# An attention and mixture-of-experts kernel on one core: memory of the last values apart, and the head of the first list gathered from a view without the last two chunks

## The chip, the cores and the metric

The kernel runs on one core of one Trainium2 chip. The metric is the device time of one execution in microseconds (us), as the median of several runs. Of the kernel before three runs are shown, and one more execution was recorded by the hardware profiler; all times of single instructions come from that one.

## The reference

```python
def _attn_ref(q, k, v, tau):                       # q, k, v: 4 x 5056 x 256
    qn = q / (np.linalg.norm(q, axis=1, keepdims=True) + 1e-06)
    kn = k / (np.linalg.norm(k, axis=1, keepdims=True) + 1e-06)
    s = kn.transpose(0, 2, 1) @ qn / tau           # 256 x 256 for each batch
    s = s - s.max(-1, keepdims=True)
    a = np.exp(s)
    a /= a.sum(-1, keepdims=True) + 1e-09
    return v @ a

def _moe_ref(x, w_gate, w1, w2):                   # x: the 20224 rows of the attention's output
    ...
    order = np.argsort(-flat)                      # flat: logits x @ w_gate, 20224 x 8
    assigned = -np.ones(N, dtype=np.int64)
    counts = np.zeros(E, dtype=np.int64)
    for idx in order:                              # each expert takes at most cap = 2528 tokens
        tok, e = (int(idx) // E, int(idx) % E)
        if assigned[tok] >= 0 or counts[e] >= cap:
            continue
        assigned[tok] = e
        counts[e] += 1
    ...
    for e in range(E):
        mask = assigned == e
        h = np.maximum(x[mask] @ w1[e], 0.0)       # 256 -> 1024
        out[mask] = h @ w2[e]                      # 1024 -> 256
```

## The kernel before

**Attention.** The tokens of a batch lie in five chunks of 1024 rows. The function `scores` multiplies keys and queries, `softmax` makes the 256 x 256 matrix a, and the value matmuls (`x_tiles`, L226, tile `px`) make the rows x = v a. One call of `x_tiles` makes a pair of 128-row tiles: matmuls into one PSUM tile `px` (pool `ps_x`, four buffers) and an eviction on ScalarE (L230). Every second pair, `store_x` (L236) stores 512 KB of rows to the DRAM tile `x_d` on ScalarE's queue. The values lie in SBUF tiles `vr` (pool `vp`, nine buffers) or in `ua` and `ub`, which later hold the experts' weights (`HOMES`).

**Routing.** The choice of tokens doesn't read `x_d`: the logits are made from values and gates on the chip and stand in L. For each expert p, `route(p)` finds the tokens: a search over the sixteen high bits of the keys and one over the low bits, four rounds each. A round is a comparison on VectorE (L635, two halves), matmuls that count (L600, L613) and some small steps on VectorE. It ends in a 0/1 mask over 128 x 160 positions, its running sum (`prefix`, L515) and the expert's number `ei`, which starts the load of the expert's weights. `compact(p)` turns the mask into a list of 20 columns of 128 token numbers: per column one matmul (L815, tile `pi`), and one test on ScalarE (L833) or VectorE (L849), for expert 0 in the ratio 11 to 9 (`NACT`); then a dozen very small steps on VectorE make `src` (the rows in `x_d`, last write L917) and `idx` (the rows of the output, L930). A column of the list is gathered by one indirect DMA of GpSimd (`fetch` in `load_x`, L1118, tile `xg`), 128 rows at a time.

**Experts.** Expert by expert, `layer1` (L1316, tile `ph`) and `layer2` (L1350, tile `py`) run over chunks of up to four columns; expert 0 has chunks of 2, 4, 4, 4, 4 and 2 columns (`FIRST_CUT`). Every number is split into a high and a low part, so that three matmuls stand for one: ScalarE writes the high part (L1319), VectorE the low part (L1324). The gathered rows are turned by `turn` (transposes L1273, one PSUM tile `pt`; high part L1275, low part L1278). Most chunks behind the third are turned through DRAM instead (`stage`, L1182 and L1184). A column's result goes from `y` to the output by an indirect DMA (L1359).

**Order.** From the value matmuls of the table `TODO` on the order on all engines is fixed by hand. An object `o` keeps a planned time of TensorE and VectorE; each matmul adds to it (`tick`), and at each tick streams of routing work put their next instruction into the queues when it is due. `o.until(key)` lets that planned time run on, without matmuls, until a stream has reached a point.

**The seam.** `TODO` names 13 chunks of four pairs, 52 pairs in all; the routing of expert 0 and the beginning of that of expert 1 run beside them. Behind them the value pools are closed and the pool `ffx` takes their place. Then the first six columns are gathered: the DRAM tile `x_d` is their source, so each gather waits for all stores. A row of 24 matmuls (L1411, `START_TICKS`) whose results nobody reads is put in TensorE's queue, then `turn(0, 0, 0)` and `turn(0, 0, 1)`, then `layer1` of the first chunk, the two turns of the second chunk, and `layer2` of the first chunk.

## Time and profile before

| what | us |
| --- | --- |
| median of three runs | 1281.18 (1277.91 to 1281.96) |
| the profiled execution, whole | 1281.94 |
| its span, first to last instruction | 1279.2 |
| TensorE busy within the span | 1253.7 |
| VectorE, ScalarE, GpSimd busy | 842.8, 551.0, 395.1 |

A busy time is the sum of the intervals in which an engine had an instruction under way. The span is made of stages with different limits, so the shares of the whole page are averages; the rows below are from the stage around the change, where the value matmuls end and the experts begin. A row of a timeline gives start, length, engine, line, operation, what is written from what, the form, and in brackets how long the engine stood idle before and what ended that. The start of a DMA row is that of the instruction that issues it. The granted clock of TensorE is 1.00 at 2.4 GHz and 0.50 at 1.2 GHz.

### The profile page before, as it was taken

The numbers are of one execution on the slowest core, as the hardware profiler recorded it, in microseconds if no ns is written. First come the engines' busy times: TensorE is split into PE (matmuls) and PEld (weight loads), VectorE is DVE, ScalarE is ACT, GpSimd is POOL, SyncE is SP. The second block draws the span as 40 slices with busy tenths as digits, with TensorE's granted clock in tenths as the row PEclk, the third lists the DMA queues.
The fourth block names the chain that finished last, engine by engine and source line by source line (L and its number), as shares of the span: only waits on it lengthen the run. The fifth ranks groups of instructions, "written<-read, shape, count | busy, mean of one in ns | idle before, by whom it ended". The sixth has DMA issues, their size and how long they took to land.

```text
span 1279.2 us, 23255 instructions
## 1 busy us (share of the span) xinstructions
PE 1253.7 (98%) x8827; PEld 1117.8 (87%) x8827; DVE 842.8 (66%) x2153; ACT 551.0 (43%) x1273; POOL 395.1 (31%) x662
## 2 busy tenths in 40 slices
PE   7999999999899999999999999999999999999998
PEld 6889877888788888998999898988988998898998
DVE  6788595889479678878866877877744334434421
ACT  5567642335234443524443553453455334334331
POOL 1000000000243363244424533453344344335322
PEclk9999999999899999999999999999999999999999
DMA  8998983344224124222422431433143235323310
GB/s 290 364 391 318 394 305 127 132 155 179 67 84 151 38 67 139 84 92 65 157 67 87 148 107 36 147 122 97 64 155 120 78 104 163 106 66 103 111 62 33
DMA packets 67119, 178.29 MB, mean 139 GB/s; under 512 B 10944, under 2 KB 33344, under 8 KB 62400
## 3 DMA queue, kind: packets, MB, share of 16 engines
q1 hardware_dynamic: 39808, 97.54, 21.5%
q0 software_dynamic: 17664, 58.22, 14.1%
q10 hardware_dynamic: 9536, 21.06, 4.2%
q8 instruction: 69, 1.13, 0.4%
q14 instruction: 42, 0.34, 0.1%
HBM read 117.53 MB, written 59.24 MB: 138 GB/s over the span
## 4 chain that ended last, share of the span: by engine, by line
PE 85%; issue 5%; DVE 5%; POOL 2%; DMA 2%; ACT 1%; POOLq 0%; SPq 0%; DVEq 0%; ACTq 0%
PE py L1350 31%; PE ph L1316 30%; PE s L305 8%; PE px L226 8%; PE pc L600 2%; PE px L269 2%; PE px L417 1%; POOL out_dram L1359 1%; DMA xg<-x_d,src 1%; DVE acc_q L315 1%; DVE acc_k L315 1%; DVE hL L1324 1%; PE pi L815 1%; DMA ua<-in_q_dram 1%; ACT hH L1319 0%
## 5 line engine op out<-in xcount | busy, mean ns | idle before, releaser
L1350 PE MATMUL py<-ua,hH 128*128 128x256 f32 (+1 forms) x2560 | 449.9, 279 | 0.0
L1316 PE MATMUL ph<-xH,ua 128*128 128x512 f32 (+3 forms) x1312 | 410.9, 388 | 3.9 <-DVE hL L1324 2.1
L1350 PEld LDWEIGHTS py<-ua,hH 128*128 128x128 f32 (+1 forms) x2560 | 388.5, 187 | 2.3
L1350 PE MATMUL py<-ua,hL 128*128 128x256 f32 (+1 forms) x1280 | 356.6, 279 | 0.0
L1324 DVE SCALAR_TENSOR_TENSOR hL<-ph,hH 128x512 fp32r<-128x512 f32 (+3 forms) x328 | 218.8, 668 | 160.1 <-ACT hH L1319 150.8
L1316 PEld LDWEIGHTS ph<-xH,ua 128*128 128x128 f32 x1312 | 244.6, 189 | 51.3 <-DVE hL L1324 4.4
L1319 ACT ACTIVATE hH<-ph 128x512 fp32r<-128x512 f32 (+3 forms) x328 | 190.8, 582 | 220.2 <-PE ph L1316 210.8
L1359 POOL DMA_INDIRECT out_dram<-y,idx x160 | 158.8, 993 | 319.9 <-ACT y L1357 281.0
L1316 PE MATMUL ph<-xL,ua 128*128 128x512 f32 (+3 forms) x656 | 254.6, 388 | 1.0 <-DVE xL L1278 0.6
L1350 PEld LDWEIGHTS py<-ua,hL 128*128 128x128 f32 (+1 forms) x1280 | 239.2, 187 | 0.0
L1118 POOL DMA_INDIRECT xg<-x_d,src x160 | 163.3, 1021 | 98.1 <-issue 45.6
L1357 ACT ACTIVATE y<-py 128x256 f32<-128x256 f32 (+1 forms) x160 | 61.4, 384 | 287.6 <-PE py L1350 247.6
L305 PE MATMUL s<-ua 128*128 128x256 f32 (+1 forms) x640 | 145.9, 387 | 6.9 <-DMA ua<-in_q_dram 6.9
L305 PEld LDWEIGHTS s<-ua 128*128 128x128 f32 (+1 forms) x640 | 122.4, 194 | 27.0 <-issue 6.4
L1316 PEld LDWEIGHTS ph<-xL,ua 128*128 128x128 f32 x656 | 124.1, 189 | 24.7 <-DVE xL L1278 2.0
L314 ACT ACTIVATE sq<-ua 128x1024 f32<-128x1024 f32 (+1 forms) x80 | 76.3, 970 | 50.4 <-DMA ua<-in_k_dram 19.3
L1204 DVE TENSOR_TENSOR xL<-xT,xH 128x512 fp32r<-128x512 f32 (+1 forms) x68 | 44.9, 678 | 64.4 <-ACT xH L1201 55.8
L1129 POOL COPY spacer<-hH 1x1 f32<-1x1 f32 x128 | 26.8, 209 | 160.8 <-ACT hH L1319 155.1
L230 ACT ACTIVATE xs<-px 128x512 f32<-128x512 f32 x60 | 35.8, 597 | 62.9 <-PE px L226 62.8
L226 PE MATMUL px<-a,vr 128*128 128x256 f32 x256 | 59.0, 384 | 0.0
L335 POOL TENSOR_SCALAR ny<-ny 128x4 f32<-128x4 f32 x4 | 2.0, 506 | 183.5 <-ACT ny L334 183.5
L226 PEld LDWEIGHTS px<-a,vr 128*128 128x128 f32 x256 | 47.1, 190 | 5.8
(298 smaller groups left out, 1358.1 us busy)
## 6 DMA issues: line engine op xcount, KB each, us to landing
x_d<-xs ACTq DMA_DIRECT2D x39, 512.0 KB
ua<-in_k_dram SPq DMA_DIRECT2D x35, 512.0 KB
ua<-in_q_dram SPq DMA_DIRECT2D x35, 512.0 KB
via<-xs SPq DMA_DIRECT2D x33, 512.0 KB
xT<-via SPq DMA_DIRECT2D x132, 128.0 KB
vr<-in_vt_dram SPq DMA_DIRECT2D x14, 1024.0 KB
ua<-in_vt_dram SPq DMA_DIRECT2D x4, 1024.0 KB
xg<-x_d,src POOLq DMA_INDIRECT x160
```

The source lines that it names most:

```text
L226: mm = PE.matmul(px[:, i * C:i * C + width], lhsT=vs[b, c][:, kb, t + i, :], rhs=a_f[b][:, kb, 0:width], start=(kb == 0), stop=(kb == 1))
L230: S.activation(xs[:, t % TH:t % TH + n, 0:width], px[:, 0:n * width].rearrange("p (t c) -> p t c", t=n), AF.Copy)
L305: newest[0] = PE.matmul(sb[:, ib * C:(ib + 1) * C], lhsT=kt[:np_, t, ib * 128:(ib + 1) * 128], rhs=qt[:np_, t, :], start=(first and t == 0 ...
L314: S.activation(sq[:n, t0:t1], t_[:n, t0:t1], AF.Square)
L1118: P.indirect_dma_start(out=xg[:n, i, :], out_offset=None, in_=x_d, in_offset=bass.IndirectOffsetOnAxis(ap=idx[:n, col:col + 1], axis=0))
L1204: V.tensor_tensor(xL[:, kb, 0:k * 128].rearrange("p (i t e) -> p i t e", i=k, t=4), rows, xH[:, kb, 0:k * 128].rearrange("p (i t e) -> p i ...
L1316: PE.matmul(ph[:, 0:nt], lhsT=l[:, w], rhs=x_[:, kb, 0:nt], start=(i == 0), stop=(i == 5))
L1319: S.activation(hH[:, fb, 0:nt], ph[:, 0:nt], AF.Relu)
L1324: V.scalar_tensor_tensor(hL[:, fb, 0:nt], ph[:, 0:nt], 0.0, hH[:, fb, 0:nt].bitcast(F32), op0=OP.max, op1=OP.subtract)
L1350: PE.matmul(py[:n, 0:C], lhsT=l[:, fb, tk], rhs=w[:, d], start=(j == 0), stop=(j == 23))
L1357: S.activation(y[:n], py[:n, 0:C], AF.Copy)
L1359: sd = P.indirect_dma_start(out=out, out_offset=bass.IndirectOffsetOnAxis(ap=idx[:n, col:col + 1], axis=0), in_=y[:n], in_offset=None)
```

## The change

Of the 52 pairs the last six (`LATE`) are put behind the end of the list of expert 0 in TensorE's queue. They belong to the chunks (3, 3) and (3, 4), which now come last in `TODO`; `ua` holds (2, 4) to (3, 2) in their place. These two chunks have value tiles of their own in a pool `vp_l`, and with them the row buffers `xs`, the matrices of the last two batches and two of the four `px` buffers are in pools that stay open (`apool_l`, `vp_l`, `ps_xl`). The other value pools are closed ahead of the last six pairs, `vp` has seven buffers and not nine, and `ffx` is opened in their place.

The list of expert 0 is made in two halves. For the first, `compact` copies the mask, clears its last 16 positions (those of the two late chunks), and makes four columns (`HEAD`) from it, with two tests on ScalarE and two on VectorE. Then it takes the 512 tokens that were listed out of the mask, and makes the other 16 columns (nine tests on ScalarE, seven on VectorE). The four columns of the head are gathered from `x_d[0:LATE_ROW]`, a view that ends ahead of the two late chunks. In TensorE's queue the order is now: five late pairs, the transposes of the first chunk in one PSUM tile (`turn_both`), the sixth pair, `layer1` of the first chunk, `layer2` of its first column, and the two turns of the second chunk within the second column. The 24 matmuls without a reader are gone. The fifth and sixth column are gathered behind the last pair from the whole of `x_d`. The tiles `hH` and `hL` of every second chunk, and the tiles of `stage`, move to a pool `ffx2` in the memory of the late values. For all experts the running sum of the mask moves from `route` to the head of `compact`, behind `ei`.

```diff
...
+LATE = 6
+LATE_ROW = (B * NCH - 2) * CH
...
+HEAD = 4
+NACT = {HEAD: 2, NCOL - HEAD: 9}
...
-BUFS_V = 9
+BUFS_V = 7
...
-         (3, 0): [(2, 2)], (3, 1): [(2, 3)], (3, 4): [(2, 4), (3, 0), (3, 1), (3, 2), (3, 3), (3, 4)]}
+         (3, 0): [(2, 2)], (3, 1): [(2, 3)], (3, 4): [(3, 3), (3, 4), (2, 4), (3, 0), (3, 1), (3, 2)]}
...
+    apool_l = lctx.enter_context(tc.tile_pool(name="apool_l", bufs=1, side="right"))
+    vp_l = lctx.enter_context(tc.tile_pool(name="vp_l", bufs=2, side="right"))
+    ps_xl = lctx.enter_context(tc.tile_pool(name="ps_xl", bufs=2, space=PSUM, side="right"))
...
-    ps_x = actx.enter_context(tc.tile_pool(name="ps_x", bufs=4, space=PSUM, side="right"))
+    ps_x = actx.enter_context(tc.tile_pool(name="ps_x", bufs=2, space=PSUM, side="right"))
...
+    def next_px():
+        px_at[0] += 1
+        return (ps_x if px_at[0] % 2 and px_at[1] else ps_xl).tile([128, 512], F32, name="px")
...
-        yield ve(COLS, 0.5)
-        r["sc"] = prefix(r["mask"], "a")
...
     def compact(p):
+        mask = routed[p]["mask"]
+        if p > 0:
+            yield ve(COLS, 0.5)
+            sc = prefix(mask, "a")
+            yield from listed(p, sc, 0, NCOL)
+            return
+        head = rtile("mem")
+        yield ve(COLS)
+        V.tensor_copy(head, mask)
+        yield ve(16)
+        V.memset(head[:, COLS - 16:COLS], 0.0)
+        yield ve(COLS, 0.5)
+        sc = prefix(head, "a")
+        yield from listed(p, sc, 0, HEAD)
+        yield ve(COLS, 2, ptr=1)
+        V.tensor_scalar(sc, sc, routed[p]["first"], None, op0=OP.add)
+        yield ve(COLS)
+        V.scalar_tensor_tensor(head, sc, HEAD * 128.0, head, op0=OP.is_le, op1=OP.mult)
+        yield ve(COLS)
+        V.tensor_tensor(head, mask, head, op=OP.subtract)
+        yield ve(COLS, 0.5)
+        sc = prefix(head, "a")
+        yield from listed(p, sc, HEAD, NCOL)
+
+    def listed(p, sc, c0, c1):
...
-            P.indirect_dma_start(out=xg[:n, i, :], out_offset=None, in_=x_d,
-                                 in_offset=bass.IndirectOffsetOnAxis(ap=idx[:n, col:col + 1], axis=0))
+            rows = x_d[0:LATE_ROW] if p == 0 and col < HEAD else x_d
+            P.indirect_dma_start(out=xg[:n, i, :], out_offset=None, in_=rows, in_offset=bass.IndirectOffsetOnAxis(
+                ap=routed[p]["src", col][:n, col:col + 1], axis=0))
...
+    def turn_both():
+        xg = xgs[0, 0]
+        ready[0, 0] = 2
+        nt = n_of(0, 0)
+        xH, xL = xts[0, 0] = (ffx.tile([128, 2, 512], F32R, name="xH"), ffx.tile([128, 2, 512], F32R, name="xL"))
+        pt = ps_t.tile([128, 512], F32, name="pt")
+        for i in range(cuts[0][0]):
+            for kb in range(2):
+                PE.transpose(pt[:, kb * nt + i * 128:kb * nt + (i + 1) * 128].bitcast(F32R),
+                             xg[:, i, kb * 128:(kb + 1) * 128].bitcast(F32R), identr)
+        for kb in range(2):
+            rows = pt[:, kb * nt:(kb + 1) * nt]
+            S.activation(xH[:, kb, 0:nt], rows, AF.Copy)
+            V.tensor_tensor(xL[:, kb, 0:nt], rows, xH[:, kb, 0:nt].bitcast(F32), op=OP.subtract)
...
-        hH = ffx.tile([128, 8, 512], F32R, name="hH")
-        hL = ffx.tile([128, 8, 512], F32R, name="hL")
+        home = (ffx, ffx2)[chunks.index((p, c)) % 2]
+        hH = home.tile([128, 8, 512], F32R, name="hH", bufs=1)
+        hL = home.tile([128, 8, 512], F32R, name="hL", bufs=1)
...
+        for at_ in pairs[:-LATE]:
+            pair(*at_)
         o.until(("ei", 0))
         settle()
         o.until(("idx", 0))
         actx.close()
         cctx.close()
...
         for c in range(2):
             load_x(0, c)
-            while queue:
-                gather()
+        head, queue[:] = list(queue), []
+        for n, at_ in enumerate(pairs[-LATE:]):
+            if n == LATE - 1:
+                queue[:] = head[:HEAD]
+                while queue:
+                    gather()
+                turn_both()
+            pair(*at_)
+        lctx.close()
+        ffx2 = ctx.enter_context(tc.tile_pool(name="ffx2", bufs=1))
+        ps_2 = ctx.enter_context(tc.tile_pool(name="ps_2", bufs=2, space=PSUM))
+        queue[:] = head[HEAD:]
+        while queue:
+            gather()
         load_x(0, 2)
+        load_ahead(0, 0)
...
-        idle = ps_1.tile([128, 512], F32, name="ph")
-        for i in range(START_TICKS):
-            o.tick(200)
-            PE.matmul(idle, lhsT=wt[0, 0][0][:, 0:128], rhs=wt[0, 0][0][:, 512:1024], start=(i == 0),
-                      stop=(i == START_TICKS - 1))
-        turn(0, 0, 0)
-        turn(0, 0, 1)
...
-                    turn(p, 1, 0)
-                    turn(p, 1, 1)
-                    layer2(p, 0, h[0], {})
+                    layer2(p, 0, h[0], {1: [turn_at(1, 0)], (1, 12): [turn_at(1, 1)]})
```

## Rows read from the trace of the kernel before

**Rows 1.** The page's first part: busy time of each engine, its share of the span, its count of instructions.
```profile
PE 1253.7 (98%) x8827; PEld 1117.8 (87%) x8827; DVE 842.8 (66%) x2153; ACT 551.0 (43%) x1273; POOL 395.1 (31%) x662
```

**Rows 2.** The busy time of each engine in five stretches (us from the span's start): the list of expert 0, the last value matmuls, the wait with the filler, the two layers of the first chunk, the rest of expert 0. The columns: the stretch, its length, the busy time of PE, PEld, DVE, ACT and POOL, each with its count of instructions (x), the granted clock of TensorE, the DMA share, GB/s.
```profile
281.00:303.30 22.30, 22.30 (x119) 19.16 (x118) 21.67 (x69) 14.85 (x45) 2.73 (x2) 1.00 0.62 236
303.30:322.25 18.95, 18.95 (x140) 16.35 (x138) 15.76 (x49) 6.94 (x14) 0.00 (x0) 1.00 0.36 144
322.26:334.74 12.48, 7.73 (x50) 5.86 (x51) 4.63 (x16) 1.25 (x3) 5.09 (x5) 0.88 0.24 77
334.74:350.80 16.06, 14.65 (x125) 14.30 (x125) 7.28 (x17) 4.95 (x12) 4.34 (x8) 0.88 0.12 35
350.80:461.00 110.20, 108.07 (x868) 97.69 (x867) 85.91 (x239) 45.39 (x126) 46.87 (x72) 1.00 0.28 90
```

**Rows 3.** The chain of waits in the stretch 318 to 352 us, in order of time: start, length, what. L600 is a step of the search for expert 1, L1316 layer 1, L1350 layer 2.
```profile
324.60 0.60 PE pc L600 x20
...
334.74 7.74 PE ph L1316 x48
...
344.70 4.40 PE py L1350 x38
349.10 0.60 PE pc L600 x20
```

**Rows 4.** Timeline of TensorE inside the first chunk: two neighbouring periods of three matmuls in layer 1 (L1316), and two in layer 2 (L1350).
```profile
341.46 0.40 PE L1316 MATMUL ph<-xH,ua 128*128 128x256 f32 x2
...
341.82 0.40 PE L1316 MATMUL ph<-xH,ua 128*128 128x256 f32 x2
...
345.31 0.39 PE L1350 MATMUL py<-ua,hH 128*128 128x256 f32 x2
...
345.65 0.39 PE L1350 MATMUL py<-ua,hH 128*128 128x256 f32 x2
```

**Rows 5.** Two short stretches, with the granted clock (columns as in the five stretches above).
```profile
332.00:334.00 2.00, 0.37 (x1) 0.18 (x1) 0.24 (x1) 0.38 (x1) 1.39 (x3) 0.50 0.35 111
...
340.00:342.00 2.00, 2.00 (x19) 2.00 (x18) 1.27 (x3) 1.00 (x4) 0.00 (x0) 1.00 0.00 0
```

**Rows 6.** Timeline of TensorE: the transposes of the first chunk, one line for each of its gathers, and the two halves of the second chunk.
```profile
331.28 0.28 PE L1273 MATMUL pt<-identr,xg 128*128 128x128 f32 x1 [1.77 <-DMA xg<-x_d,src]
332.94 0.37 PE L1273 MATMUL pt<-identr,xg 128*128 128x128 f32 x1 [1.37 <-DMA xg<-x_d,src]
...
342.30 0.46 PE L1273 MATMUL pt<-identr,xg 128*128 128x128 f32 x4
344.17 0.53 PE L1273 MATMUL pt<-identr,xg 128*128 128x128 f32 x4 [1.41 <-DVE xL L1278]
```

**Rows 7.** Timeline of ScalarE and of its queue: evictions (L230) and stores (L236) of the last value tiles.
```profile
306.70 0.33 ACTq L236 DMA_DIRECT2D x_d<-xs  x1
...
310.37 0.60 ACT L230 ACTIVATE xs<-px 128x512 f32<-128x512 f32 x1
...
320.56 0.60 ACT L230 ACTIVATE xs<-px 128x512 f32<-128x512 f32 x1
...
322.29 0.60 ACT L230 ACTIVATE xs<-px 128x512 f32<-128x512 f32 x1 [1.13 <-PE px L226]
322.91 0.33 ACTq L236 DMA_DIRECT2D x_d<-xs  x1
```

**Rows 8.** Timeline of GpSimd: the first two gathers of x, one instruction for each 128 rows of the list.
```profile
328.43 0.95 POOL L1118 DMA_INDIRECT xg<-x_d,src  x1 [43.63 <-DVE cur L663]
329.69 1.40 POOL L1118 DMA_INDIRECT xg<-x_d,src  x1 [0.30 <-issue]
```

**Rows 9.** The DMA share in two half microseconds behind the last store (columns as above).
```profile
324.00:324.50 0.50, 0.50 (x5) 0.23 (x4) 0.00 (x0) 0.00 (x0) 0.00 (x0) 1.00 1.09 352
...
326.00:326.50 0.50, 0.50 (x4) 0.39 (x3) 0.09 (x1) 0.00 (x0) 0.00 (x0) 1.00 0.08 12
```

**Rows 10.** Timeline of SyncE's queue: a store of 512 KB to DRAM (L1182) and the loads that wait for it (L1184).
```profile
374.58 0.33 SPq L1182 DMA_DIRECT2D via<-xs  x1
378.19 1.79 SPq L1184 DMA_DIRECT2D xT<-via  x4
```

**Rows 11.** Timeline of VectorE: the scan that opens the list of expert 0, the last step of that list, the first comparison of the search for expert 1, and a comparison beside a gather.
```profile
280.94 0.49 DVE L515 TENSOR_TENSOR_SCAN sc_a<-ones_r,mk 128x160 f32<-128x160 f32 x1
...
303.10 0.17 DVE L917 COPY_PREDICATED src<-early,w__2660 128x20 int32<-128x20 int32 x1
...
305.82 0.78 DVE L635 TENSOR_TENSOR ge<-hi,th 128x1200 bf16<-128x1200 int16 x1
...
329.48 0.78 DVE L635 TENSOR_TENSOR ge<-low,th 128x1200 bf16<-128x1200 int16 x1
```

**Rows 12.** The instructions on the tile pi: the tests of the list of expert 0 that run on ScalarE (duration ns min/median/max, first and last start in us).
```profile
L833 ACT ACTIVATE junk<-pi,rhalf x11: 385/392/395, 284.8 to 298.5; 128x160 bf16<-128x160 f32 x11
```

**Rows 13.** The first and the fourth round of the low half of the search for expert 1 (timeline of TensorE, two rounds lie between), the last write of the list of expert 1 (the line L917), and the first transposes of its x (timeline of TensorE).
```profile
348.94 0.76 PE L600 MATMUL pc<-oh,ge 128*128 128x64 bf16 x20
...
380.18 0.76 PE L600 MATMUL pc<-oh,ge 128*128 128x64 bf16 x20
...
L917 DVE COPY_PREDICATED src<-early,w__4241 x1: 184/184/184, 430.2 to 430.2; 128x20 int32<-128x20 int32 x1
...
458.44 0.45 PE L1273 MATMUL pt<-identr,xg 128*128 128x128 f32 x4
```

More of the change, by code (lines that the diff above doesn't have):

```diff
@@ L56 @@
 PAD_W = 8
+PAD_X = 16
 PAD_H = 24
@@ L916, in compact @@
-        yield ve(NCOL)
-        V.copy_predicated(src, early, w3_)
-        r["src"] = src
-        r["time"] = o.pe
-        done["idx", p] = True
-        lists.append(p)
+        yield ve(nc_)
+        V.tensor_tensor(w3_[:, cs_], w2_[:, cs_], at[:, cs_], op=OP.add)
+        yield ve(nc_)
+        V.copy_predicated(src[:, cs_], early[:, cs_], w3_[:, cs_])
+        for col in range(c0, c1):
+            r["src", col] = src
+        if not short:
+            r["time"] = o.pe
+            done["idx", p] = True
+            lists.append(p)
@@ L934, in attention_moe @@
+        if not short:
+            done["out", p] = True
     reading = []
@@ L1170, in stage @@
         if half == 0:
[L1171 removed]
+            moved[p, c] = (ffx2.tile([128, 1024], F32, name="xs", bufs=1), ffx2.tile([128, 1024], F32, name="xT", bufs=1))
         xs, xT = moved[p, c]
```

160 lines of the change are left out of this document (84 added, 76 removed).

## The prediction

> **What bounds the kernel now.** I read the page's first part, then the busy time by stretches around the seam, then the chain of waits across it. TensorE is busy 98% of the span [rows 1]. In the stretches of the list and of the last value matmuls it has no idle time at all, and behind the first chunk it stands idle 2.1 of 110.2 us; in the wait it is busy 7.7 of 12.5 us, and nearly all of that is the filler [rows 2]. So the kernel is bound by TensorE's work, and what is taken out of TensorE's empty time at the seam comes off the end, as long as no list is late further on. The chain shows what the seam consists of: last eviction, last store, gather, transposes, layer 1 at a low rate, turns, layer 2 [rows 3, 6, 7, 8].
>
> How much is empty? From the end of the last value matmul (322.26) to the first matmul of the second chunk (350.80) are 28.54 us. The work in it: layer 1 has 48 matmuls at 0.36 us for three, 5.76 us; layer 2 has 48 at 0.34 for three, 5.44 [rows 4]; twelve transposes at 0.46 for four, 1.38 [rows 6]; two steps of the search at 0.60, 1.20 [rows 3]. Sum 13.78, so 14.76 us are empty or slow. Within them layer 1 took 7.74 us [rows 3], 1.98 more than its 5.76: the granted clock was 0.50 at 332 to 334 us, behind a stretch with little work, and 1.00 again at 340 to 342 [rows 5].
>
> **The change part by part.** *Late pairs in place of the wait.* The 24 filler matmuls, the wait for the last store and the gathers, and the half clock go. That is the 14.76 us, from which I take what comes back.
>
> Does the new order cover the gathers of the first chunk? The head's gathers need the store of the last early chunk's rows, (2, 3). In today's order that is the 44th pair, whose store is issued at 306.70 [rows 7]. From a store to the first gather that waits for it took 5.52 us at the seam (322.91 to 328.43) [rows 7, 8]; another 512 KB store let its load start after 3.61 us [rows 10]. The seam's one carries a stray: its bulk moved by 324.5, and a little piece at 326.0 to 326.5 [rows 9]. So the first head gather starts between 310.3 and 312.2. From a gather's start to the transposes that use it were 2.85 and 3.25 us, and the second starts 1.26 us behind the first [rows 6, 8], so the second column is there by 314.8 to 316.7. TensorE reaches the transposes five pairs behind the 46th, which ended at 310.3; a pair is 1.73 us [rows 7], so not before 319. Hidden, with 2 to 4 us to spare; if that cover were gone, each missing microsecond would be lost, and the clock with it.
>
> *The high and low parts of the first chunk* are made beside the sixth late pair. Both halves together have as many columns as one half of the second chunk, and there activation and subtraction took 1.41 us from the end of the transposes to the release [rows 6]. The pair gives 1.73 us of cover; ahead can stand the rest of an eviction of 0.60 us on ScalarE [rows 7] and half a comparison, 0.78 us, on VectorE [rows 11]. Bounds 0 and 1.5 us; I take 0.3, near the covered case.
>
> *Two lists.* VectorE was busy 21.67 of 22.30 us while the list was made [rows 2], from 280.94 to 303.28 [rows 11]. Added are some six wide steps at up to 0.49 us and some sixteen small ones at up to 0.17 [rows 11], 5.7 us at the most; they overlap a little, and I take 4. The head, with a fifth of the tests and all the fixed steps of a list, should be there near 289, 8 us behind the scan. The other half has nine of the eleven tests on ScalarE, which took 13.7 us from first to last start, 1.37 each [rows 12], so 11 us for nine, with 5 to 6 us ahead and behind: near 306. Between the bounds of 303.3 (today's) and 312 (the head, then all of today's 22.3 us again) the 46th pair ends at 310: cost 0 to 2 us, I take 0. The two small matmuls that a second list adds cost TensorE 0.25 us, an estimate from a lone transpose of 0.28 [rows 6], since they are narrow too and follow each other.
>
> *The search of expert 1* begins some 4 us later, at about 310 in place of 305.82 [rows 11]. Its matmuls are TensorE work wherever they run, so moving a round from the pairs into the experts costs nothing by itself. Its comparisons now stand on VectorE among the low parts of the first chunks: 0 to 1.5 us, I take 0.5.
>
> *Fifth and sixth column.* Now only these wait for the last store. Last pair to store issue is 0.66 us (322.25 to 322.91) [rows 7], then 3.6 to 5.5 us, then 1.26 and 2.85 to 3.25: they are there 8.4 to 10.7 us behind the last pair. They are needed after layer 1 (5.76) and one column of layer 2 (2.72), at 8.48. Cost 0 to 2.2 us; I take 0.5, nearer to the store without a stray. Behind these gathers GpSimd's queue holds the first result's scatter and the third chunk's gathers, which are not due yet.
>
> *Turns of the second chunk.* Today the second half waits for the first's low part, 1.87 us behind it [rows 6], so the two cost 2.4 us up to layer 2. Twelve matmuls of layer 2 between them now give 1.36 us of cover, and an eviction of `y` stands ahead on ScalarE. Bounds 0 and 1.0; I take 0.5.
>
> *Fewer value buffers, other order of loads, `ffx2`, the running sum for other experts:* nothing. A gain is excluded where TensorE has no idle time, and it has none in the stretches where the values are read [rows 2]; the h tiles keep two buffers, and the running sum is the same instruction in another place. A late value tile would cost what TensorE then waits; 0 to 1 us, I take 0.
>
> Sum: 14.76 - 0.3 - 0.25 - 0.5 - 0.5 - 0.5 = 12.7 us. Against the profiled execution's own 1281.94 (a span of 1279.2 and 2.7 around it) that is 1269.2; that execution stood 0.8 above the median shown, so I name 1269.2 without moving it.
>
> **A rule against it.** The second gather began at 329.69, 0.21 us into a comparison on VectorE that took 0.78, and its instruction took 1.40 us; the first, without one, took 0.95 [rows 8, 11]. The six gathers now all run while the search is under way. So each could take 0.45 us more: for the fifth and sixth together 0.9, on the path where they are already late, and the time 1270.1. The Trainium skill (SBUF — State Buffer, section "Who interferes with whom") says that GpSimd and VectorE in its two-port modes lock each other out of a shared port pair, and that DMAs issued by GpSimd wait with it. [...]
>
> **The rivals.**
> (a) *The list of expert 1 is late, and the gain is given back at the border of experts 0 and 1; slower than before if far enough.* By the start of layer 1 today all four high rounds of that search are done; after the change I count two, with a third possible under the first column's layer 2. A round among expert matmuls is 10.4 us (348.94 to 380.18 for three) [rows 13]. Today the list is written at 430.2 and its rows are turned at 458.4 [rows 13], 28 us; four gathers and a landing take 6.6 to 7, and the first chunk gets 3.4 us shorter (1.98 of clock, 1.4 of turns), so some 17.6 us are free. One round late, 10.4: nothing. Two, 20.8: 3.2 us lost, 1272.4. Two and a half with the 4 us of VectorE, 30: 12.4 lost, 1281.6. It is slower than before from a delay of 30.3 us on, and three rounds with the 4 us would give 17.6 lost, 1286.8. For it: rounds beside experts are nearly twice as long as the 5.9 us beside value matmuls and filler (305.82 to 329.48 for four [rows 11]). Against: the round that began at 329.48 today reached its matmuls only at 348.94 [rows 11, 13], so the seam holds up the search too, and the new order gives that time back.
> (b) *The view doesn't part the gathers from the late stores.* Then the head waits for the store behind the 50th pair, issued near 318; the second column comes at 326 to 328 where TensorE wants it at 319 to 320: 6 to 8 us of stall and 2 of half clock again. Gain 3 to 5, near 1278.
> (c) *The second list ends behind the early pairs* by the bound of 312 or more, and the last gathers hit a stray as today's did: 2 lost there, 1.7 more for the fifth and sixth column, 1 for VectorE behind it, 1273.9.
>
> **How the numbers follow.** The forecast (1267 to 1271.5) gets 0.66; the gathers beside the search, inside that range too, 0.06; (c) and the mild part of (a), 1272 to 1277, 0.12; (b), and (a) at a small gain or none, 0.11; (a) beyond 30 us, slower, 0.05. The range from 1266.5 to 1277 leaves out about 0.16 with a little below. A measurement here can tell about 0.3%, 3.8 us, from no change. Faster by more, below 1277.3: 0.85. Within: 0.10. Slower: 0.05.
>
> **What would show it.** Right: no L1411, no gap over 1 us in TensorE between value matmuls and the first chunk, granted clock 1.00 there, layer 1 of the first chunk near 5.8 us, head gathers near 311, the second chunk's first matmul near 336 to 338, with two of the search's rounds moved behind the start of layer 1. Wrong: transposes of the first chunk waiting for gathers (b); L917 of expert 0 behind 310 (c); waits of TensorE at the border of experts 0 and 1 with L917 of expert 1 near its transposes (a); or new waits for values ahead of 280 us, where I put nothing.

## The result, and the profile after

The kernel after takes 1293.19 us (median of 4 runs, 1290.80 to 1294.63); the kernel before, beside it, 1281.45 (1277.91 to 1281.96). The ratio is 1.0099, with an interval of 1.0074 to 1.0123: **slower by about 1%**, 11.7 us, where 12 us less were forecast. The profiled execution took 1294.63, with a span of 1292.8.

The page's first part, to be read beside [rows 1]:

```profile
PE 1268.0 (98%) x8821; PEld 1127.5 (87%) x8821; DVE 845.8 (65%) x2178; ACT 551.2 (43%) x1273; POOL 399.0 (31%) x658
```

TensorE executes nearly as many matmuls as before (8821 against 8827: the 24 fillers are gone, 16 transposes and two small matmuls of the second list are new), but is busy 14.3 us longer, and the span is 13.6 us longer. So on balance the loss is not idle time: the matmuls take longer, some of them all the time, some while the clock is at half. A share of busy time (98% in both) cannot show that.

Was it the seam? The timeline of TensorE there, from the transposes of the first chunk (L1341) over layer 1 (L1380) and layer 2 (L1413) to the second chunk:

```profile
321.43 0.65 PE L1341 MATMUL pt<-identr,xg 128*128 128x128 f32 x4
...
323.63 0.47 PE L1380 MATMUL ph<-xH,ua 128*128 128x256 f32 x1
...
326.64 0.39 PE L1380 MATMUL ph<-xH,ua 128*128 128x256 f32 x1 [0.50 <-DVE hL L1388]
...
330.31 0.40 PE L1413 MATMUL py<-ua,hH 128*128 128x256 f32 x2
...
333.14 0.46 PE L1319 MATMUL pt<-identr,xg 128*128 128x128 f32 x4
...
336.20 0.51 PE L1319 MATMUL pt<-identr,xg 128*128 128x128 f32 x4 [0.52 <-DVE xL L1324]
...
338.14 0.39 PE L1380 MATMUL ph<-xH,ua 128*128 128x512 f32 x1
```

No. The transposes wait for nothing, and the second chunk begins at 338.14 in place of 350.80: 12.66 us are gained there. They are lost later. Setting the starts of the layers in the two traces side by side gives where (us; the border runs from layer 2 of the last two chunks of expert 0 to layer 1 of the third chunk of expert 1):

| stretch | before | after | difference |
|---|---|---|---|
| up to the second chunk of expert 0 | 350.80 | 338.14 | -12.66 |
| from there to layer 2 of its last two chunks | 92.79 | 92.71 | -0.08 |
| border of experts 0 and 1 | 56.38 | 64.89 | +8.51 |
| up to layer 1 of expert 4 | 323.36 | 327.33 | +3.97 |
| that layer 1 (two chunks) | 24.88 | 28.74 | +3.86 |
| from there to the end | 430.99 | 440.99 | +10.00 |

Two kinds of loss: two places, and a steady one. In the second row the steady one is hidden: TensorE is busy 1.73 us longer there (92.39 for 90.66), but idle only 0.32 us in place of 2.13. It is seen best where nothing else happens, in one chunk of the last expert. The starts of a layer 1, of the layer 2 behind it and of the next layer 1, before:

```profile
1198.70 0.40 PE L1316 MATMUL ph<-xH,ua 128*128 128x512 f32 x1
...
1209.65 0.40 PE L1350 MATMUL py<-ua,hH 128*128 128x256 f32 x2
...
1220.56 0.40 PE L1316 MATMUL ph<-xH,ua 128*128 128x512 f32 x1
```

and after:

```profile
1210.19 0.39 PE L1380 MATMUL ph<-xH,ua 128*128 128x512 f32 x1
...
1221.37 0.40 PE L1413 MATMUL py<-ua,hH 128*128 128x256 f32 x2
...
1232.68 0.39 PE L1380 MATMUL ph<-xH,ua 128*128 128x512 f32 x1
```

48 matmuls of layer 1 took 10.95 us and now take 11.18; 96 of layer 2 took 10.91 and now take 11.31. There are no waits in it and the clock is 1.00. For one matmul (of 512 columns in layer 1, of 256 in layer 2) that is 228.1 to 232.9 ns (2.1%) and 113.6 to 117.8 ns (3.7%). The durations in the rows (0.39, 0.40) hide it, because matmuls overlap; only the distance of starts shows it.

The two places, as stretches with the busy time of PE, PEld, DVE, ACT and POOL, the granted clock, the DMA share and GB/s: layer 2 of the last two chunks of expert 0, layer 1 of the first two of expert 1, layer 2 of its first (these three are the border), and layer 1 of the first two of expert 4. Before:

```profile
443.59:462.51 18.92, 18.92 (x196) 18.88 (x195) 12.61 (x41) 5.63 (x15) 10.44 (x15) 1.00 0.20 65
462.51:488.06 25.55, 25.05 (x149) 19.63 (x148) 21.30 (x48) 12.76 (x24) 13.91 (x20) 1.00 0.33 98
488.06:499.97 11.91, 11.91 (x120) 11.88 (x118) 9.60 (x37) 3.16 (x8) 4.49 (x9) 1.00 0.27 93
823.33:848.21 24.88, 23.92 (x132) 19.06 (x130) 20.58 (x47) 18.05 (x58) 12.79 (x19) 1.00 0.51 166
```

After:

```profile
430.85:453.38 22.53, 20.63 (x196) 20.30 (x195) 12.81 (x50) 5.41 (x14) 10.61 (x15) 0.92 0.17 59
453.38:483.12 29.74, 26.61 (x128) 20.37 (x127) 21.29 (x46) 13.10 (x25) 17.34 (x23) 0.94 0.32 97
483.12:495.74 12.62, 12.62 (x139) 12.53 (x138) 8.37 (x27) 3.04 (x7) 5.59 (x10) 1.00 0.32 113
823.07:851.81 28.74, 26.82 (x145) 21.17 (x145) 22.72 (x49) 17.78 (x51) 13.69 (x20) 0.94 0.39 130
```

At both places TensorE stands idle for 1.9 to 3.1 us, and the mean clock falls to 0.92 to 0.94. What it waits for, and the matmuls behind a wait that come at about half the rate (462.03 to 463.31, three matmuls in 1.28 us in place of 0.70):

```profile
445.70 0.37 PE L1319 MATMUL pt<-identr,xg 128*128 128x128 f32 x3
447.97 0.37 PE L1319 MATMUL pt<-identr,xg 128*128 128x128 f32 x1 [1.90 <-DMA xg<-x_d,src]
...
457.99 0.28 PE L1319 MATMUL pt<-identr,xg 128*128 128x128 f32 x1 [0.94 <-DMA xg<-x_d,src]
459.24 0.28 PE L1319 MATMUL pt<-identr,xg 128*128 128x128 f32 x1 [0.97 <-DMA xg<-x_d,src]
460.51 0.28 PE L1319 MATMUL pt<-identr,xg 128*128 128x128 f32 x1 [0.99 <-DMA xg<-x_d,src]
...
462.03 1.05 PE L1380 MATMUL ph<-xH,ua 128*128 128x512 f32 x2
...
463.31 1.05 PE L1380 MATMUL ph<-xH,ua 128*128 128x512 f32 x2
...
835.88 0.54 PE L1319 MATMUL pt<-identr,xg 128*128 128x128 f32 x4 [1.93 <-ACT ext L922]
```

The lists of experts 0 (head and rest) and 1 are written here:

```profile
L959 DVE COPY_PREDICATED src_h<-early,w__2532 x1: 165/165/165, 288.8 to 288.8; 128x4 int32<-128x4 int32 x1
L959 DVE COPY_PREDICATED src<-early,w__2750 x1: 181/181/181, 309.9 to 309.9; 128x16 int32<-128x16 int32 x1
L959 DVE COPY_PREDICATED src<-early,w__4452 x1: 185/185/185, 433.0 to 433.0; 128x20 int32<-128x20 int32 x1
```

and GpSimd issues the head's gathers and, later, the four of the first chunk of expert 1 so:

```profile
312.56 1.20 POOL L1164 DMA_INDIRECT xg<-x_d,src_h  x1 [28.94 <-DVE bt L971]
...
435.81 1.16 POOL L1164 DMA_INDIRECT xg<-x_d,src  x1 [0.30 <-DVE ua L1143]
...
438.65 0.98 POOL L1164 DMA_INDIRECT xg<-x_d,src  x1 [0.30 <-issue]
...
442.29 0.98 POOL L1164 DMA_INDIRECT xg<-x_d,src  x1 [0.30 <-issue]
...
444.94 1.23 POOL L1164 DMA_INDIRECT xg<-x_d,src  x1 [0.30 <-issue]
```

The list of expert 1 is 2.8 us later than before (430.2 [rows 13]), while TensorE is 12.7 us earlier. And its gathers don't follow one another: one goes out behind the scatter (the store of a result to the output) of each column of layer 2.

### The profile page after: what moved, and what is told of

The parts are those of the page before. It is cut to its first block, busy times and chain, and to the rows that moved or that the text cites. A ratio compares the mean times of both kernels' runs of the same rounds, so it can differ in the third digit from the quotient of the medians.

```text
span 1292.8 us, 23226 instructions
## 1 busy us (share of the span) xinstructions
PE 1268.0 (98%) x8821; PEld 1127.5 (87%) x8821; DVE 845.8 (65%) x2178; ACT 551.2 (43%) x1273; POOL 399.0 (31%) x658
## 4 chain that ended last, share of the span: by engine, by line
PE 85%; issue 5%; DVE 4%; POOL 3%; DMA 1%; ACT 1%; DVEq 0%; POOLq 0%; SPq 0%; ACTq 0%
PE py L1413 31%; PE ph L1380 30%; PE s L320 8%; PE px L241 7%; PE pc L615 2%; PE px L284 2%; POOL out_dram L1424 2%; PE px L432 1%; DMA xg<-x_d,src 1%; POOL xg L1164 1%; DVE acc_q L330 1%; DVE acc_k L330 1%; PE pi L856 1%; DMA ua<-in_q_dram 0%; PE pt L1319 0%
## 5 line engine op out<-in xcount | busy, mean ns | idle before, releaser
L1413 PE MATMUL py<-ua,hH 128*128 128x256 f32 (+1 forms) x2560 | 462.3, 282 | 0.0
L1380 PE MATMUL ph<-xH,ua 128*128 128x512 f32 (+3 forms) x1312 | 415.5, 392 | 2.9 <-DVE xs L1223 2.4
L1413 PEld LDWEIGHTS py<-ua,hH 128*128 128x128 f32 (+1 forms) x2560 | 392.3, 187 | 2.3
L1413 PE MATMUL py<-ua,hL 128*128 128x256 f32 (+1 forms) x1280 | 358.2, 280 | 0.0
L1380 PEld LDWEIGHTS ph<-xH,ua 128*128 128x128 f32 x1312 | 245.1, 189 | 53.4 <-DVE xs L1223 3.2
L1380 PE MATMUL ph<-xL,ua 128*128 128x512 f32 (+3 forms) x656 | 256.3, 391 | 0.4 <-DVE xL L1324 0.2
L1413 PEld LDWEIGHTS py<-ua,hL 128*128 128x128 f32 (+1 forms) x1280 | 238.7, 186 | 0.0
L1380 PEld LDWEIGHTS ph<-xL,ua 128*128 128x128 f32 x656 | 124.2, 189 | 25.7 <-DVE xL L1250 1.1
L1250 DVE TENSOR_TENSOR xL<-xT,xH 128x512 fp32r<-128x512 f32 (+1 forms) x64 | 42.3, 678 | 60.7 <-ACT xH L1247 55.0
L241 PE MATMUL px<-a,vr 128*128 128x256 f32 x224 | 51.6, 383 | 0.0
L330 DVE TENSOR_TENSOR acc_k<-acc_k,sq 128x1024 f32<-128x1024 f32 (+2 forms) x40 | 44.2, 1111 | 8.9 <-ACT sq L329 7.7
```

The lines of the kernel that those rows point to most:

```text
L241: mm = PE.matmul(px[:, i * C:i * C + width], lhsT=vs[b, c][:, kb, t + i, :], rhs=a_f[b][:, kb, 0:width], start=(kb == 0), stop=(kb == 1))
L330: V.tensor_tensor(acc[:n, t0:t1], acc[:n, t0:t1], sq[:n, t0:t1], op=OP.add)
L1250: V.tensor_tensor(xL[:, kb, 0:k * 128].rearrange("p (i t e) -> p i t e", i=k, t=4), rows, xH[:, kb, 0:k * 128].rearrange("p (i t e) -> p i ...
L1380: PE.matmul(ph[:, 0:nt], lhsT=l[:, w], rhs=x_[:, kb, 0:nt], start=(i == 0), stop=(i == 5))
L1413: PE.matmul(py[:n, 0:C], lhsT=l[:, fb, tk], rhs=w[:, d], start=(j == 0), stop=(j == 23))
```

## The experiments

**Theory A** for the steady loss: the feed-forward tiles lie elsewhere in SBUF, and that sets the period of the matmuls. In the built program the addresses of xg, xH, xL, hH and hL moved, and within 256 bytes per partition each of them by 128 (64 bytes are `pad_x`, a tile that nothing reads and that the change adds at L1468; 64 are the routing's new tiles). The PSUM tiles pt and py changed banks. **Rivals**: the banks (B), the order of the h tiles among themselves (C). **Theory D** for the border: the list of expert 1 is late for TensorE, and the gathers' pace makes it worse; rivals: it hangs on GpSimd's queue (E), or another wait takes its place (F). Each ratio is against runs of the kernel before on the same chip; their medians there were 1277.4 (e1 to e4), 1279.8 (e5 to e9), 1279.5 (e10 to e13) and 1277.6 (e14 to e16). A ratio as recorded can differ from the quotient of the two medians by up to 0.13%.

**Only the place.** e1_before_all_ff_128B, the kernel before:

```
+        ffx.tile([128, 32], F32, name="pad_x", bufs=1)
```

> The kernel before, with one tile of 128 bytes per partition put first into the pool ffx, so that xg, xH, xL, hH, hL, y and xT all lie 128 bytes further on; same instructions in the same order. Theory A (the place of the feed-forward tiles in SBUF sets the matmul period; the change moved them by 128 bytes): three matmuls of layer 2 take 0.352 us in place of 0.341 behind 1080 us, six of layer 1 0.70 in place of 0.683, and the time goes up by 13 to 24 us, to 1294 to 1305. Rival B (the PSUM banks of pt and py set the period): no change, 1280 to 1283. Rival C (the order of the h tiles among themselves sets it): no change.

1291.26 us, ratio 1.0117 (1.0100 to 1.0134). No instruction is changed and no wait is new, and the chunk shown above takes 11.19 and 11.31 us, as in the kernel after:

```profile
1203.81 0.39 PE L1316 MATMUL ph<-xH,ua 128*128 128x512 f32 x1
...
1215.00 0.40 PE L1350 MATMUL py<-ua,hH 128*128 128x256 f32 x2
...
1226.31 0.39 PE L1316 MATMUL ph<-xH,ua 128*128 128x512 f32 x1
```

So 128 bytes cost 1.17% of 1277.4, 14.9 us (13.8 by the medians): more than the whole change was to bring.

**The banks.** e3_before_banks, the kernel before:

```
+        ps_t = ctx.enter_context(tc.tile_pool(name="ps_t", bufs=1, space=PSUM))
         ps_2 = ctx.enter_context(tc.tile_pool(name="ps_2", bufs=2, space=PSUM))
-        ps_t = ctx.enter_context(tc.tile_pool(name="ps_t", bufs=1, space=PSUM))
```

> The kernel before with the pool ps_t opened ahead of ps_2, so that pt lies in PSUM bank 5 and py in 6 and 7, as in the kernel after; SBUF as before. Theory A: no change, 1280 to 1283, periods 0.341 and 0.683. Rival B: period of layer 2 0.352, time 1290 to 1305. Rival C: no change.

1277.38 us, ratio 1.0004 (0.9993 to 1.0015). B falls: other banks make no difference.

**The change with the old place.** e4_after_pad_112 and, after the period was known, e16_after_pad_48:

```
-PAD_X = 16
+PAD_X = 112
```

and 48 in e16.

> The kernel after with pad_x of 112 words in place of 16, so that the tiles of ffx and ffx2 have the offset within 512 bytes that they have in the kernel before; PSUM and order as after. Theory A, if it is the offset within 512 bytes that counts: 0.341 and 0.683 again, and the time falls by 13 to 24 us from 1293, to 1269 to 1280. Rivals B and C: no change, 1291 to 1295.

> The kernel after with pad_x of 48 words in place of 16, so that x and h lie 256 bytes further on than in the kernel before. If the place repeats every 256 bytes in this kernel too, the periods are 0.341 and 0.683, and the ratio is that of the pad of 112 words, 0.996 to 1.001; if not, it stays near 1.010.

1276.37 us, ratio 0.9998 (0.9986 to 1.0010), and 1277.17, 0.9999 (0.9986 to 1.0012). In both the chunk takes 10.94 and 10.92 us, here in e4:

```profile
1193.31 0.40 PE L1380 MATMUL ph<-xH,ua 128*128 128x512 f32 x1
...
1204.25 0.40 PE L1413 MATMUL py<-ua,hH 128*128 128x256 f32 x2
...
1215.17 0.40 PE L1380 MATMUL ph<-xH,ua 128*128 128x512 f32 x1
```

C falls too, since the order of the h tiles is that of the kernel after. So one word count in a pad takes 1.0% off the time of the kernel after, and with the tiles at the old place the change is worth nothing that can be measured: all of the seam's gain is used up elsewhere.

e4 also shows that the half clock doesn't come behind every wait. TensorE waits 1.94 us there for a gather at the border, and 1.96 us in expert 4, and the granted clock stays at 1.00 behind both; it is 0.50 only behind the three waits for the second chunk (0.93, 1.02 and 0.92 us, up to 458.00). Rows of TensorE's timeline, and stretches with the columns as above:

```profile
446.93 0.28 PE L1319 MATMUL pt<-identr,xg 128*128 128x128 f32 x1 [1.94 <-DMA xg<-x_d,src]
446.93:450.00 3.07, 3.07 (x41) 3.00 (x42) 1.37 (x4) 0.60 (x1) 0.94 (x2) 1.00 0.26 85
...
459.00:462.00 3.00, 3.00 (x9) 2.33 (x8) 2.02 (x4) 1.11 (x2) 2.53 (x4) 0.50 0.38 109
...
827.70 0.53 PE L1319 MATMUL pt<-identr,xg 128*128 128x128 f32 x4 [1.96 <-ACT ext L922]
827.70:832.00 4.30, 4.30 (x22) 3.64 (x23) 2.48 (x6) 1.79 (x3) 3.80 (x7) 1.00 0.79 293
```

**Which tiles, and how far.** On the kernel before, e2_before_h_128B (h alone), e5_before_x_128B (x alone; h moves by 512) and e12_before_all_ff_256B (all, twice as far), in this order:

```
-PAD_H = 24
+PAD_H = 56
```

```
-PAD_H = 24
+PAD_H = 120
...
+        ffx.tile([128, 32], F32, name="pad_x", bufs=1)
```

```
+        ffx.tile([128, 64], F32, name="pad_x", bufs=1)
```

> The kernel before with pad_h 128 bytes longer, so that only hH, hL, y, xs and xT lie 128 bytes further on, while xg, xH and xL stay; same instructions. Theory A: layer 2, which reads hH and hL, goes to 0.352 us for three, layer 1 stays at 0.683 for six, and the time goes up by 9 to 16 us, to 1290 to 1297. If it is where x lies that counts, layer 1 alone would not change and neither would layer 2: 1281. Rivals B and C: no change.

> The kernel before with 128 bytes ahead of xg, xH and xL, and 384 more ahead of the h tiles, so that x lies 128 bytes further on (as in the kernel after) and hH and hL lie 512 further, at their old offset within 512. Theory A1 (each layer's period hangs on the offset of its own tiles): layer 1, which reads x, goes to 0.70 us for six matmuls, layer 2, which doesn't, stays at 0.341 for three; 320 groups of six at 0.017 more are 5.5 us, so a ratio of 1.003 to 1.005 to before. Theory A2 (the pace of layer 1 is carried into the layer 2 behind it): layer 2 goes to 0.353 too in the phases that follow layer 1, and the ratio is 1.009 to 1.012. If the offset within 512 isn't what counts, both layers may change in another way.

> The kernel before with 256 bytes ahead of all tiles of ffx, twice the shift that cost 1.17%. Theory A-256 (what counts repeats every 256 bytes): periods 0.341 and 0.683 as before, ratio 0.999 to 1.001. Theory A-512 (it repeats every 512 bytes, and other offsets are slow): periods near 0.352 and 0.70, ratio 1.005 to 1.015.

Ratios 1.0035 (1.0023 to 1.0048), 1.0039 (1.0029 to 1.0049), 1.0001 (0.9988 to 1.0014). A shift by 256 bytes changes nothing, moving x slows layer 1 and moving h slows layer 2, and the sum of the parts is less than the whole. e2 was to cost 9 to 16 us and cost 3.5 by the medians: its layer 2 was slow in part of the phases only.

**Place or distance.** On the kernel before, e14_before_w2_and_ff_128B (the first edit: the weights of layer 2 move with x and h) and e15_before_w2_128B (both edits: within 256 bytes, those weights alone):

```
-PAD_W = 8
+PAD_W = 40
...
+        ffx.tile([128, 32], F32, name="pad_x", bufs=1)
```

> The kernel before with pad_w 128 bytes longer: the weights of layer 2 (ua2, ua3), the raw weights, the routing's tiles and all of ffx lie 128 bytes further on; only the weights of layer 1 (ua0, ua1) stay. Theory R (what counts is the distance, within 256 bytes, between the two operands that TensorE reads): layer 1 is slow (0.70 for six), since x moved and its weights didn't; layer 2 stays at 0.341, since h and its weights moved together; ratio 1.003 to 1.006. Theory P (the place of x and h itself counts): both layers slow, as with all of ffx 128 bytes further, 0.70 and 0.353, ratio 1.010 to 1.014.

> The same, with 128 more bytes ahead of ffx, so that x and h lie 256 bytes further on than before, and of the operands of the two layers only the weights of layer 2 have another offset within 256 bytes. Theory R: layer 1 at 0.683, layer 2 slow in some or all phases (0.352), ratio 1.003 to 1.008. Theory P: no change, 0.999 to 1.001.

Ratios 1.0066 (1.0049 to 1.0082) and 1.0049 (1.0032 to 1.0066). All together, with the offsets of the tiles within 256 bytes (w1, w2: the weights of the two layers) and the times of one layer 1 and one layer 2 of the last expert, read from the distance of starts as in the fences above:

| kernel | w1 | x | w2 | h | layer 1, us | layer 2, us | ratio |
|---|---|---|---|---|---|---|---|
| before, e3, e12 | 32 | 32 | 64 | 128 | 10.94 to 10.95 | 10.91 to 10.92 | 1, 1.0004, 1.0001 |
| after | 32 | 160 | 64 | 0 | 11.18 | 11.31 | 1.0099 |
| e1 | 32 | 160 | 64 | 0 | 11.19 | 11.31 | 1.0117 |
| e2 | 32 | 32 | 64 | 0 | 10.95 | 10.88 | 1.0035 |
| e5 | 32 | 160 | 64 | 128 | 11.15 | 10.90 | 1.0039 |
| e14 | 32 | 160 | 192 | 0 | 11.15 | 10.92 | 1.0066 |
| e15 | 32 | 32 | 192 | 128 | 10.90 | 11.30 | 1.0049 |
| e4, e16 (after) | 32 | 32 | 64 | 128 | 10.94 | 10.92 | 0.9998, 0.9999 |

Layer 1 is slow in each case where x lies 128 bytes from where it was; no run moves w1, so for layer 1 it isn't shown whether x's own place counts or its distance from w1. In layer 2, e15 speaks against the place of h alone: h is where it was, only w2 moved, and these are the three rows of its chunk:

```profile
1203.05 0.39 PE L1316 MATMUL ph<-xH,ua 128*128 128x512 f32 x1
...
1213.95 0.40 PE L1350 MATMUL py<-ua,hH 128*128 128x256 f32 x2
...
1225.25 0.39 PE L1316 MATMUL ph<-xH,ua 128*128 128x512 f32 x1
```

But distance alone does not tell everything. From expert 5 on, layer 2 of e2 is slow (0.352 us for three matmuls) only in the last two chunks of each expert, and that of e15 everywhere but there. In e14, where h and w2 kept their distance, it is slow from the end of expert 5 through the first three chunks of expert 6, fast in those of expert 7, and slow again in its last two. Even the kernel before isn't always fast: from expert 5 on all of its layer 2 runs at the fast pace, but earlier some of it runs at the slow one, as in the second chunk of expert 2, where three matmuls take 0.35 to 0.36 us:

```profile
633.03 0.40 PE L1350 MATMUL py<-ua,hH 128*128 128x256 f32 x2
...
633.39 0.40 PE L1350 MATMUL py<-ua,hH 128*128 128x256 f32 x2
```

So up to expert 4 there was less to lose, which fits the smaller loss in that row of the first table. What sets the pace of layer 2, and hands it from one phase to the next, stays open.

**The border: turn later.** e6_after_pad_turns_late, on e4:

```
-            h[0] = layer1(p, 0, {} if p == 0 else {2: [turn_at(1, 0)], 7: [turn_at(1, 1)], **pieces})
+            h[0] = layer1(p, 0, {} if p == 0 else {5 if p == 1 else 2: [turn_at(1, 0)], 7: [turn_at(1, 1)], **pieces})
```

> The kernel after with pad_x of 112 words, and for expert 1 alone the first transposes of the second chunk three groups of layer 1 later (18 matmuls, 4.1 us). Theory D (the border of experts 0 and 1 costs what TensorE waits for gathers there and the half clock behind it; three of the waits are on this chunk): the waits of 0.93, 1.02 and 0.92 us and the 2.2 us of half clock behind them go, 4 to 5 us, so 1271 to 1272.5 where the pad alone has 1276.4. Rival E (the gathers only come later in turn, or another wait takes their place): 1275 to 1277.

1275.51 us, ratio 0.9959 (0.9944 to 0.9975). By the two ratios that is 0.4% better than e4, by the two medians 0.9 us: the kernel before, to which each is set, was 2.3 us slower on this chip. The waits for the second chunk's gathers are gone; the one of 1.91 us for the first chunk is still there, and here the clock is 0.50 behind it (446 to 449 us).

**The border: two gathers for each column.** e11_after_pad_two_gathers, on e4:

```
-            if queue and left(*queue[0][0]) < URGENT:
-                gather()
+            for _ in range(2):
+                if queue and left(*queue[0][0]) < URGENT:
+                    gather()
```

> The kernel after with pad_x of 112 words, and up to two gathers in place of one behind each scatter of a column. Theory D2 (the first rows of expert 1 come late because one gather goes out for each column of layer 2, so the four took 14.7 us from the list to the last landing and not the 7 that four in a row would take): the wait of 1.94 us goes and the gathers of the second chunk start 5 us earlier, so the waits there and the half clock shrink too; 4 to 6 us, ratio 0.995 to 0.997. Rival E (GpSimd's queue or the list itself sets it): ratio 0.999 to 1.001.

1277.52 us, ratio 0.9978 (0.9968 to 0.9987). All four waits for gathers are gone, as D2 has it, and the ratio lies between its range and that of rival E: 3.00 of their 4.8 us come back as a wait of TensorE for a step of the next search:

```profile
443.71 0.32 PE L628 MATMUL pc<-Ex,ones_q 128*128 128x96 f32 x1 [3.00 <-DVE Dr L621]
```

**The border: the list earlier.** The planner puts a step of a search into TensorE's order only when it is a margin of 700 ns behind its planned release. e7_after_pad_margin0 sets 0 for all experts, e9_after_pad_margin0_e0 for expert 0 alone, e10_after_pad_margin350_e0 350 ns for expert 0; all on e4:

```
-        o.margin = MARGIN
+        o.margin = 0
...
+            if p == 1:
+                o.margin = MARGIN
```

(e7 without the last two lines, e10 with 350 for 0.)

> The kernel after with pad_x of 112 words and a margin of 0 in place of 700 ns for all experts, so that the steps of the searches stand earlier in TensorE's order (the tests of the list of expert 1 end 15 matmuls of layer 1 and 96 of layer 2 earlier, some 14 us of work). Theory D: the waits at the border of experts 0 and 1 go, 7 us; all lists are earlier. Rival F (TensorE then waits for VectorE at the steps of every search, up to 0.7 us each): the gain is lost to new waits, and the time is 1276 or longer.

> The same with the margin of 0 only while expert 0 runs, so only the search for expert 1 is moved ahead. Theory D: the waits of 1.94, 0.93, 1.02 and 0.92 us at the border and the half clock go, 6.5 to 7 us, minus some waits for VectorE in that one search: 1270 to 1272. Rival F: 1275 or longer.

> The kernel after with pad_x of 112 words and a margin of 350 in place of 700 ns while expert 0 runs. With 700 the border of experts 0 and 1 had waits for gathers of 4.8 us and half clock behind them; with 0 these went, but TensorE waited 4.2 us for VectorE in that one search. Theory D with F (two prices against each other, the smaller sum lies between): the list of expert 1 stands some 8 us of TensorE's work earlier than with 700, half of the waits at the border go and a third of the waits for VectorE come: ratio to before 0.990 to 0.994. If the ratio is that of the margin of 700 (0.9998), the waits at the border don't hang on the list.

1286.16 us, ratio 1.0044 (1.0032 to 1.0057); 1272.81, **0.9933** (0.9914 to 0.9951); 1278.85, 0.9997 (0.9985 to 1.0010). e9's time lies 0.8 us above its range. Its list of expert 1 is written at 416.4 in place of 432.2 (e4), and TensorE waits for no gather at the border. It waits for VectorE in that search instead, 4.2 us in the six longest waits, of which these are two:

```profile
406.04 0.42 PE L615 MATMUL pc<-oh,ge 128*128 128x48 bf16 x10 [1.33 <-DVE ge L650]
...
450.09 0.32 PE L628 MATMUL pc<-Ex,ones_q 128*128 128x96 f32 x1 [0.95 <-DVE Ex L624]
```

With 0 for all experts such waits go on beside the later experts, and it is slower than before (F). The value between, e10, missed its forecast: it has new waits of 1.20 and 2.07 us for low parts and one of 2.58 for a search step. The order that the planner writes does not change smoothly with the margin.

**All three.** e13_after_pad_mixed: margin 350, two gathers, later turn.

> The kernel after with pad_x of 112 words, a margin of 350 ns while expert 0 runs, two gathers behind each scatter, and the first transposes of the second chunk of expert 1 three groups of layer 1 later. Theory D: nothing waits at the border of experts 0 and 1, so the gain of the seam, 9 to 12 us, is kept but for 1 to 3 us of waits for VectorE: ratio 0.990 to 0.994, provided that no new wait turns up at a later border. Rival E: ratio above 0.996.

1274.33 us, ratio 0.9959 (0.9947 to 0.9971), short of D's range. Nothing waits for gathers at the border, but there are waits of 1.20 and 2.13 us in expert 0, and e9 is better. e9 beats both kernels: 0.7% under before (0.5% by the medians), 1.6% under after by the two ratios (0.9933 / 1.0099 = 0.9836).

What did the repairs bring at the border itself? The distance from the start of the second chunk of expert 0 to layer 1 of the third chunk of expert 1, and TensorE's idle time in it (us, one profiled execution each, tiles at the old place):

| kernel | from | to | distance | idle |
|---|---|---|---|---|
| e3 (kernel before) | 347.36 | 494.61 | 147.25 | 1.61 |
| e4 | 338.36 | 492.45 | 154.09 | 5.72 |
| e6, turn later | 337.01 | 490.35 | 153.34 | 4.28 |
| e11, two gathers | 337.68 | 489.94 | 152.26 | 4.05 |
| e9, margin 0 | 338.49 | 491.20 | 152.71 | 4.26 |
| e10, margin 350 | 338.22 | 495.35 | 157.13 | 7.22 |
| e13, all three | 338.11 | 491.46 | 153.35 | 5.10 |

e4 loses 6.84 us there against e3 (some 0.6 of it a search step of 20 matmuls [rows 3] that now stands in this stretch), and the repairs bring back 0.7 to 1.8; e10 loses more. So D is shown for the waits, which go when the gathers or the list come earlier, but not for the time: other waits take their place, as F has it. The rest of e9's lead is elsewhere: its profiled span is 3.2 us under e4's (1270.6 and 1273.8), of which 1.4 come from this stretch.

## Why the prediction was wrong

**The seam: the mechanism right, the match partly luck.** The filler, the wait for the last store and the half clock went; 12.66 us by the start of the second chunk, where 12.7 was the sum. The head's gathers begin at 312.56 (310.3 to 312.2 was said) and are hidden: the transposes at 321.43 wait for nothing. The second list ends at 309.9, inside 303.3 to 312. The second chunk's turn waits 0.52 us (0.5 taken). In smaller terms: no wait for xL (0.3 taken) and none for the fifth and sixth column (0.5), but 0.50 for a low part in layer 1, and 1.65 for the new lists' small steps (0.66 at 291.46, 0.99 at 294.66), where I had taken 0 of a bound of 2. And 40 matmuls of the search for expert 1, 1.2 us by [rows 3], now stand behind the start of the second chunk (220 are ahead of it in place of 260), so part of the gain there is work put off. That the sum came out to 0.04 us is luck. Nor is the half clock, 3.4 us of the 14.76, always there: in the profile of e3, the same instructions with two PSUM pools changed over, the second chunk starts at 347.36 and not 350.80, and where the clock was 0.50 [rows 5] it is 1.00:

```profile
332.00:334.00 2.00, 1.69 (x10) 1.29 (x11) 0.55 (x2) 0.39 (x1) 1.53 (x2) 1.00 0.41 131
```

It is 1.00 there in e1, e2 and e14 too, and 0.50 in e5, whose second chunk starts at 350.45; what decides it is open. Against e3, e4's gain at the seam is 9.0 us and not 12.7, and a ratio to the kernel before may hang on how often its clock fell there.

Of the head's gathers the first, which starts 0.40 us into a comparison, took 1.20 us and the other three 0.95, all covered; the fifth and sixth, which the rule against the forecast charged with 0.9 us, took 0.94 each with no comparison beside them. The two-port rule that the prediction sets beside this does not bear on it: the Trainium skill (SBUF — State Buffer, section "Who interferes with whom") names no two-port mode for a TENSOR_TENSOR, which the comparison is; it lets it contend with GpSimd's reads where both inputs lie in SBUF. Whether that slowed the gather, no run shows. Rivals (b) and (c) did not occur.

**The step that failed first: "Fewer value buffers, other order of loads, `ffx2`, the running sum for other experts: nothing".** This item puts the rest of the change at nothing. I looked for a price in waits and buffers, and excluded one because TensorE has no idle time; where the feed-forward tiles come to lie is in no term. A hint stood in the source: `pad_w` (L202) and `pad_h` (L1300) of the kernel before are tiles that nothing reads, so all that they do is shift addresses, and the change adds `pad_x`. I took the periods of [rows 4] as properties of the matmul. They are properties of the matmul *and of where its operands lie*. The same tiles 128 bytes further on cost 1.17% in the kernel before (e1), and putting them back takes 1.0% off the kernel after (e4, e16). With this one term, taken from e1, the sum would have been 12.7 gained and 14.9 lost: no change that can be measured.

The Trainium skill (TensorE: Matmul & The Clock Gate, section "Wait — 56ns, not 53.3ns?") gives back-to-back matmuls the time of their columns at 2.4 GHz and about 2.5 ns. That would be, as an estimate from that page, 215.8 ns in layer 1 and 109.2 in layer 2. The trace doesn't agree at either place: 228.1 and 113.6 at the old one, 232.9 and 117.8 at the new one, all at a granted clock of 1.00 and with a weight load for every matmul (8821 of either).

**The step that failed second: the price of rival (a).** The mechanism was named, and the list of expert 1 is late: 2.8 us in time, and 12.7 more because TensorE comes earlier, 15.5 together. I had counted 17.6 as free and so forecast no loss up to there. Measured is a loss of 8.5 us over the border (6.8 with the tiles at the old place: e4 is 9.0 ahead of e3 at the second chunk and 2.2 at layer 1 of the third chunk of expert 1). The mis-sized term is "four gathers and a landing take 6.6 to 7". They took 15.0 us, from 433.0 to 447.97, because each is issued behind the scatter of another column; e11 shows it by issuing two, and its waits for gathers go. With 15.0 in that sum 9.6 us are free and 5.9 are lost (an estimate). Two terms were left out: the next chunk's gathers, which queue behind (three waits, 2.9 us, gone in e6), and the half clock, which came behind both groups of waits in the kernel after and behind one of them in e4. It had a chance of 0.05 for slower; the free time should have been taken from the pace at which gathers are issued, not from their own length.

**What is only partly settled.** The stall of 1.93 us in layer 1 of expert 4 (transposes waiting for ScalarE's L922, which reads the tile that the transposes need) with the clock behind it is most of the 3.86 us there. It is there in after, e4, e6, e11 and e16, at another border in e10 (1.96 at 712.08), and not in e9 or e13; in these three the searches stand in another order. I put it down to how the steps happened to fall, but no run tests it alone. At the border it is shown where the time goes, and by which term the price was too small; no run wins back more than 1.8 of the 6.8 us, so what the border would cost without any wait is open.

## What to carry to other kernels

A change of memory layout can have a price even where no instruction changes: note the offsets of the operands of the inner matmuls within 256 bytes before and after, and if they moved, put them back with a pad before judging anything else. Time gained in a program whose lists come from another engine can be lost again where the next list is due: price that due time by the pace at which its transfers are issued, allow for half clock behind the waits (it came behind some and not others), and expect that moving the lists ahead turns the wait for data into one for the engine that makes them. And look for a loss that you mean to remove in more than one profile: the half clock at this seam, 3.4 us, was in some and not in others.

## What the runs showed of the hardware

At a granted clock of 1.00 and with no wait shown, a float32 matmul of 512 columns took 228 or 233 ns by where x lay, and one of 256 columns 113.6 or 117.8, depending on where h and the weights of layer 2 lay but not on that alone; a shift of all tiles by 256 bytes made no difference (1.0001), one by 128 made 1.17%. Other PSUM banks for pt and py made none (1.0004). Layer 2 can run a whole phase at either pace with the same addresses (before, e2, e14, e15), which I had not expected and cannot explain. The granted clock at the same seam of the same instructions was 0.50 in one execution and 1.00 in another (the profile before and e1), and behind waits of 1.9 us it fell in some cases (447.97 in the kernel after) and not in others (446.93 in e4).
